# First loads of an attention and FFN kernel in another order, staging of its own at the change of parts, and smaller DMA packets for w_out's forms

## The chip, the cores and the metric

One core of a Trainium2 chip runs the whole program. TensorE (PE) multiplies, VectorE (DVE) and ScalarE (ACT) work on tiles element by element, GpSimd (POOL) sets constants, SyncE (SP) issues most DMAs; 16 DMA engines move the data between HBM and SBUF. Times are device microseconds (us) of one execution. The kernel before took 885.45, 887.29 and 890.8 us, median 887.29.

## The reference

Linear attention without softmax, an RMS norm over each head's 64 values, and a feed-forward layer:

```python
kv = np.einsum('bhsd,bhse->bhde', k, v)          # q, k, v: 8 batches x 8 heads x 576 x 64
out = np.einsum('bhsd,bhde->bhse', q, kv)
rms = np.sqrt(np.mean(out * out, axis=-1, keepdims=True) + 1e-06)
x = (out / rms * g_norm), heads side by side      # 4608 tokens x 512
h = x @ w_in                                      # w_in 512 x 2048
g = h * np.tanh(np.log1p(np.exp(h)))              # mish
y = g @ w_out                                     # w_out 2048 x 512
```

`w_in` and `w_out` arrive as float64 and are joined to float32 on the chip from their two 32-bit words.

## The kernel before

Every float32 product is three passes over a high and a low part in `float32r` (`split`: ACT casts, DVE subtracts). Both FFN products are cut into two by two blocks that need seven products instead of eight; A11, S1, S2, S4, A12, S3, A22 are the seven left forms, T1 to T4 and B11, B21, B22 the right ones.

**Part 1** goes over 9 tiles of 512 tokens. For each it loads q, multiplies it with the batch's k/v matrix, normalizes (giving x), makes the forms of x, and multiplies with w_in in 4 groups (n = 0 to 3) of 7 products. Mish of the result goes to a DRAM tile `gd`. Meanwhile it loads k and v of the coming batches (`k_load`, in pairs p of heads, two staging tiles in turn), and makes the forms of w_out, which wait in the DRAM tiles `wod`. **Part 2** goes over 18 groups of 256 tokens: loads g from `gd`, makes its forms, and multiplies with the forms of w_out (`wo`, eight tiles that take the places of w_in's). The first of these groups is multiplied in four quarters, each with two of the eight tiles, since these arrive one after the other.

**What sets the order.** One product is one slot; a table (`at(t, f)`, run by `slot`) says behind which slot's product each other step is issued, `then` puts an eviction ahead of a product. Tile i's group n begins at slot 28 i + 7 n. Each engine runs its instructions in that order, each DMA queue too. All DMAs of SP and ACT share eight landing semaphores in turn, so each DMA also waits until the one eight before it has landed (the waits DMAHW0 to DMAHW7 in the rows below).

**The start** (lines 588 to 645) is written out by hand. w_in comes in 8 groups j of 512 KB x 2; `weights(j, LOAD, SCALE, JOIN, DIFF, BLOCKS, SUMS)` are the steps of one. Raw words wait in a tile `w64` (groups 0, 4, 7) or in a place of w_in's own (`wf5`, `wf6`, `wf7`; groups 5 and 6 reuse the places of 2 and 3, so their loads wait until DVE has joined these). The rows of q of tile 0 (`rows_load`, 4 loads of 1,024 pieces of 256 bytes), k and v of batch 0 (`kv_first`, two halves) and g_norm (`gcol`) are loaded between them on SP. The units u = 0, 1 of tile 0 (four heads each) are transposed by PE from these rows, copied (`turned`), projected, squared, summed and normalized.

**The change of parts.** At slot 6 of the last tile part 1's pools close; at slots 7 and 8 the first two groups of g are loaded, at 10, 17, 24 and 28 two w_out tiles each (a row of `wod` is 14,336 bytes in one piece per partition). ACT stores the last tile's results (`ula`, `ulb`, `ur`: the blocks 11, 21 and the right half, two buffers of each); in all tiles before, SP does. At slot 18 all seven forms of g's first quarter are made at once, in tiles of their own (`g0`).

## Time and profile before

| | |
|---|---|
| median of 3 runs | 887.29 us (885.45 to 890.8) |
| profiled execution | 885.97 us, span 884.2 us |
| granted TensorE clock, mean | 0.987 |
| PE busy | 828.1 us (94% of the span) |
| DVE, ACT busy | 608.7 us (69%), 464.6 us (53%) |
| DMA | 175.52 MB, mean 199 GB/s |

In a row of the timeline stand the start and length in us, the engine, the line, the operation, what it writes and reads, how many instructions were merged (x), and in brackets the engine's idle time before it with what ended it. SPq and ACTq are DMA issues. q1 is SP's DMA queue, q10 ACT's; behind them stand packets, MB and the time that the packets took as a share of 16 engines' time. PE is TensorE's multiplications. Part 1 ends with the product before 512 us, part 2 follows.

### The profile page before, as it was taken

What the parts mean: (1) busy time and instruction counts of PE and PEld (TensorE: products, weight loads), DVE (VectorE), ACT (ScalarE), POOL (GpSimd) and SP (SyncE); (2) the same over time, 40 slices, a digit from 0 to 9 for tenths busy, and PEclk for the clock granted to TensorE, in tenths of its full rate; (3) what the DMA queues carried; (4) which work ended last, traced back from release to release, by engine and by line L of the source; (5) the groups of instructions that cost most, each with busy time, mean ns of one, the idle gap of its engine ahead of it and who ended that gap; (6) DMA issues with size and microseconds to landing.
All of it is one profiled execution on the core that took longest, in us unless ns stands there. A gap on an engine that the chain in (4) does not pass through costs nothing.

```text
span 884.2 us, 17156 instructions
## 1 busy us (share of the span) xinstructions
PE 828.1 (94%) x7036; PEld 795.7 (90%) x7036; DVE 608.7 (69%) x804; ACT 464.6 (53%) x703; POOL 4.8 (1%) x23
## 2 busy tenths in 40 slices
PE   4658998998999999999999899999999999999997
PEld 3447898998999999999999789999999999999997
DVE  5869675886777676787764368867777677776772
ACT  3647666556675765666664444344444434434431
POOL 2000000000000000000000000000000000000000
PEclk9969999999999999999999999999999999999999
DMA  9936787987978696767477993344434443334421
GB/s 294 247 114 197 200 274 246 278 263 226 296 219 278 218 304 199 220 204 227 151 227 249 425 416 125 122 150 152 148 121 133 130 120 120 119 120 141 153 65 48
DMA packets 161038, 175.52 MB, mean 199 GB/s; under 512 B 24704, under 2 KB 142464, under 8 KB 159936
## 3 DMA queue, kind: packets, MB, share of 16 engines
q1 hardware_dynamic: 158208, 170.23, 61.8%
q10 hardware_dynamic: 2752, 4.20, 1.3%
q8 instruction: 55, 0.90, 0.4%
q14 instruction: 23, 0.19, 0.1%
HBM read 112.39 MB, written 62.00 MB: 197 GB/s over the span
## 4 chain that ended last, share of the span: by engine, by line
PE 63%; DMA 11%; DVE 10%; ACT 9%; issue 4%; SPq 2%; ACTq 0%; DVEq 0%
PE a L772 22%; PE bc L772 16%; PE a L527 13%; PE bc L527 7%; DMA gd<-ula 5%; PE s L252 2%; DMA vm<-in_v_dram 2%; DVE ur L548 1%; DMA wod<-wst 1%; ACT L412 1%; ACT gf L121 1%; DMA rd<-fl 1%; DVE gf L122 1%; DVE fa L122 1%; ACT L118 1%
## 5 line engine op out<-in xcount | busy, mean ns | idle before, releaser
L772 PE MATMUL a<-wf,gf 128*128 128x256 f32 x1632 | 201.8, 283 | 0.5 <-DVE ur L812 0.5
L772 PEld LDWEIGHTS a<-wf,gf 128*128 128x128 f32 x1632 | 198.4, 192 | 0.7 <-DVE ur L812 0.7
L122 DVE TENSOR_TENSOR gf<-g,gf 128x1024 fp32r<-128x1024 f32 (+1 forms) x123 | 132.9, 1087 | 90.7 <-ACT gf L121 90.7
L527 PE MATMUL a<-gf,wf 128*128 128x256 f32 x1296 | 173.0, 287 | 11.5 <-DVE gf L430 4.5
L527 PEld LDWEIGHTS a<-gf,wf 128*128 128x128 f32 x1296 | 162.9, 193 | 18.1 <-ACT ur L504 6.6
L527 PE MATMUL bc<-gf,wf 128*128 128x256 f32 x1296 | 170.3, 285 | 3.5 <-ACT ur L495 2.4
L527 PEld LDWEIGHTS bc<-gf,wf 128*128 128x128 f32 x1296 | 161.4, 191 | 5.1 <-ACT ur L495 2.6
L121 ACT CAST gf<-g 128x1024 fp32r<-128x1024 f32 (+1 forms) x123 | 114.6, 939 | 93.3 <-DVE g L752 65.1
L772 PE MATMUL bc<-wf,gf 128*128 128x256 f32 x1224 | 152.7, 283 | 1.0 <-DVE gf L122 1.0
L772 PEld LDWEIGHTS bc<-wf,gf 128*128 128x128 f32 x1224 | 149.4, 192 | 1.4 <-ACT gf L121 0.7
L527 PE MATMUL a<-a,wf 128*128 128x256 f32 x432 | 59.8, 289 | 2.5 <-DVE ur L548 2.5
L527 PEld LDWEIGHTS a<-a,wf 128*128 128x128 f32 x432 | 55.8, 195 | 5.6 <-DVE ur L548 3.1
L118 ACT ACTIVATE ur<-ur 128x1024 f32<-128x1024 f32 x36 | 38.1, 1059 | 37.1 <-DVE ur L548 37.1
L122 DVE TENSOR_TENSOR fa<-fl,fh 128x1024 fp32r<-128x1024 f32 x28 | 34.3, 1224 | 22.1 <-ACT fh L121 21.2
L504 ACT COPY ur<-a 128x512 f32<-128x512 f32 (+1 forms) x53 | 27.3, 516 | 37.6 <-PE a L772 24.6
L122 DVE TENSOR_TENSOR gf<-gf 128x512 fp32r<-128x512 f32 x45 | 30.4, 689 | 24.0 <-ACT gf L121 24.0
L121 ACT CAST gf<-a 128x1024 fp32r<-128x1024 f32 x17 | 17.9, 1052 | 53.5 <-DVE a L749 50.9
L121 ACT CAST gf<-gf 128x512 fp32r<-128x512 f32 x45 | 27.1, 618 | 31.4 <-DVE gf L451 19.1
L495 ACT COPY ur<-bc 128x512 f32<-128x512 f32 (+1 forms) x53 | 27.4, 517 | 29.9 <-PE bc L772 23.0
L548 DVE TENSOR_TENSOR ula<-bc,ula 128x512 f32<-128x512 f32 x36 | 24.8, 688 | 25.4 <-PE bc L527 25.3
L118 ACT ACTIVATE ula<-ula 128x512 f32<-128x512 f32 x36 | 22.8, 633 | 22.1 <-DVE ula L548 22.1
L252 PE MATMUL s<-vm,km 128*64 128x64 f32 x448 | 20.1, 235 | 14.1 <-DMA vm<-in_v_dram 14.1
(137 smaller groups left out, 858.1 us busy)
## 6 DMA issues: line engine op xcount, KB each, us to landing
g<-gd SPq DMA_DIRECT2D x18, 2048.0 KB, 8.9
gd<-ur SPq DMA_DIRECT2D x32, 512.0 KB, 4.0
wod<-wst SPq DMA_DIRECT2D x16, 896.0 KB, 5.6
wf<-wod SPq DMA_DIRECT2D x8, 1792.0 KB, 16.2
gd<-ula SPq DMA_DIRECT2D x32, 256.0 KB, 5.1
gd<-ulb SPq DMA_DIRECT2D x32, 256.0 KB, 4.3
w<-in_moe_w_out_dram SPq DMA_DIRECT2D x32, 256.0 KB, 4.6
km<-in_k_dram SPq DMA_DIRECT2D x28, 256.0 KB, 4.8
```

The source lines that it names most:

```text
L118: nc.scalar.activation(o, i, AF.Mish)
L121: nc.scalar.copy(hi, src)
L122: nc.vector.tensor_sub(lo, src, hi.bitcast(F32))
L252: nc.tensor.matmul(kvps[o * D:(o + 1) * D, b % 2, h0 // 2 + i, :], kt, vt, start=(c == 0), stop=(c == CM))
L412: nc.scalar.preload_act_table_set("natural_log_exp_and_others")
L495: then(t + 2, lambda: nc.scalar.copy(dst(st, "22"), st["c"]))
L504: then(t + 4, lambda: nc.scalar.copy(dst(st, "12"), st["a"]))
L527: nc.tensor.matmul(bank[:, jj], w[:, right, a, kc, :], xf[:, b, kc, :], start=first and jj == kc == s == 0, stop=(kc == 1 and s == 2), ski ...
L548: nc.vector.tensor_add(o, bank, o)
L772: nc.tensor.matmul(bank, gf[:, a, c, :], wo[c][:, right, b, :], start=first and c == s == 0, stop=(c == NF2 - 1 and s == 2), skip_group_ch ...
```

## The change

It has five places. (1) w_in's groups 6 and 7 are loaded two slots later, group 4 only behind the rows of tile 1. (2) q's rows of tile 0 are issued by ACT and g_norm by POOL, and at the start `turned` of unit 1 and the first k/v product with `kv_keep` move ahead. (3) The last group of the last tile gets staging of its own (`up2`). (4) The forms of g's first quarter are made one per slot, 17 to 23, in rooms of the common pool. (5) A row of `wod` gets 64 bytes behind its two halves of each form, so that w_out's forms are read in 7 pieces of 2,048 bytes per partition; each half of `wod`'s forms is stored in two DMAs.

```diff
@@ -109,7 +109,7 @@
     ones = const.tile([P, P], F32, name="ones")
     sel = const.tile([P, NKC, H], F32R, name="sel")
     gd = [tc.dram_tile([P, NFC, T], F32, name=f"gd{i}") for i in range(NT)]
-    wod = [tc.dram_tile([P, 7, 2, G], F32, name=f"wod{c}") for c in range(NF2)]
+    wod = [tc.dram_tile([P, 7, 2 * G + 16], F32, name=f"wod{c}") for c in range(NF2)]
     rd = [tc.dram_tile([H, T], F32, name=f"rd{j}") for j in range(NT)]
 
     ctx.enter_context(tc.manual_schedule(engines=None))
@@ -197,7 +197,8 @@
             return pools["w64"].tile([P, 4, P, 2], U32, name="w64")
 
         def store(f):
-            nc.sync.dma_start(wod[c][:, :, :, h * P:(h + 1) * P], f.rearrange("p f s m n -> p f s (m n)").bitcast(F32))
+            for s in range(2):
+                nc.sync.dma_start(wod[c][:, :, s * G + h * P:s * G + (h + 1) * P], f[:, :, s, 0, :].bitcast(F32))
         srcs = []
         for fh in range(2):
             f0 = (c + fh * NF2) * P
@@ -286,13 +287,13 @@
             segs.append((j, 0, slice(n, T)))
         return segs
 
-    def rows_load(j, c):
+    def rows_load(eng, j, c):
         for b, s0, cols in segments(j):
             t0, t1 = max(cols.start, c * P), min(cols.stop, (c + 1) * P)
             if t0 < t1:
                 src = q[b, 0:1, s0 + t0 - cols.start:s0 + t0 - cols.start + 1, :]
                 src = bass.AP(src.tensor, src.offset, [[D, t1 - t0], [S * D, H], [1, D]])
-                nc.sync.dma_start(rows[j][t0 - c * P:t1 - c * P, c, :].rearrange("p (h d) -> p h d", d=D), src)
+                eng.dma_start(rows[j][t0 - c * P:t1 - c * P, c, :].rearrange("p (h d) -> p h d", d=D), src)
 
     rows = {}
     qs, ss = {}, {}
@@ -534,7 +535,8 @@
 
         name, shape = {"11": ("la", TH), "21": ("lb", TH)}.get(block, ("r", T))
         if name not in st:
-            st[name] = up.tile([P, 2, shape], F32, name="u" + name)
+            pool = pools["up2"] if (st["i"], st["n"]) == (NT - 1, NQ - 1) else up
+            st[name] = pool.tile([P, 2, shape], F32, name="u" + name)
         return st[name] if name != "r" else st[name][:, :, (int(block[0]) - 1) * TH:int(block[0]) * TH]
 
     def put_in(st, block, bank, t):
@@ -590,15 +592,14 @@
     t = wfp.tile([P, 3, 2 * T], F32, name="wf2")
     rows[0], turned_q = t[:, 0:2].rearrange("p a (c n) -> p (a c) n", c=TR // 2), t[:, 2].rearrange("p (a t) -> p a t", a=2)
     for c in range(TR):
-        rows_load(0, c)
+        rows_load(nc.scalar, 0, c)
     kv0 += [wfp.tile([P, NKC, 9 * D], F32, name=f"wf{n}") for n in (3, 4)]
     kv_first(first)
     weights(1, LOAD)
     kv_first(second)
     for r in (slice(0, D), slice(D, P)):
-        nc.sync.dma_start(gcol[r, :], g_norm.rearrange("(p o) -> p o", o=1))
+        nc.gpsimd.dma_start(gcol[r, :], g_norm.rearrange("(p o) -> p o", o=1))
     weights(2, LOAD)
-    weights(4, LOAD)
     weights(3, LOAD)
     make_identity(nc, ident)
     kv_tiles()
@@ -616,11 +617,11 @@
     do(0, 1, "transpose")
     weights(0, BLOCKS)
     do(0, 0, "turned")
+    do(0, 1, "turned")
     weights(0, SUMS)
-    do(0, 1, "turned")
-    weights(1, SCALE, JOIN)
     kv_first_product(first)
     kv_keep(0, first)
+    weights(1, SCALE, JOIN)
     do(0, 0, "project", "square")
     weights(1, DIFF, BLOCKS)
     kv_first_product(second)
@@ -633,7 +634,7 @@
     k_load(1, 1)
     rows[1] = att.tile([P, TR, H * D], F32, name="qs")
     for c in range(TR):
-        rows_load(1, c)
+        rows_load(nc.sync, 1, c)
     do(0, 1, "square", "sums")
     weights(2, SCALE)
     do(0, 0, "normalize")
@@ -642,6 +643,7 @@
     do(0, 1, "rstd", "normalize")
     x_form(S1)
     weights(2, DIFF)
+    weights(4, LOAD)
     weights(5, LOAD)
 
 
@@ -651,7 +653,7 @@
     for j in range(3, NF2):
         t = 3 * (j - 3) + 1
         if j < 5:
-            at(t, lambda j=j: weights((6, 7)[j - 3], LOAD))
+            at(t + 2, lambda j=j: weights((6, 7)[j - 3], LOAD))
         for s, n in ((SCALE, 0), (JOIN, 0), (DIFF, 1), (BLOCKS, 1), (SUMS, 2)):
             at(t + n, lambda j=j, s=s: weights(j, s))
 
@@ -713,17 +715,17 @@
 
     def part2():
         part1.close()
-        open_pools(ctx, ("gp", 2), ("fp2", 1), ("g0", 1))
+        open_pools(ctx, ("gp", 2), ("fp2", 1), ("g0", 1), ("up2", 1))
         pools["ps"] = ctx.enter_context(tc.tile_pool(name="ps_u", bufs=1, space=PSUM, reuse_waits="tile"))
 
     def gf_room():
         nonlocal rooms_made
         rooms_made += 1
-        return (fp if rooms_made % 5 != 1 else pools["fp2"]).tile([P, 4, 2, 2, P], F32R, name="gf")
+        return (fp if rooms_made % 5 != 2 else pools["fp2"]).tile([P, 4, 2, 2, P], F32R, name="gf")
 
     def wo_load(c):
         wo[c] = wfp.tile([P, 7, 2, G], F32R, name=f"wf{c}")
-        nc.sync.dma_start(wo[c].bitcast(F32), wod[c])
+        nc.sync.dma_start(wo[c].bitcast(F32).rearrange("p f s n -> p f (s n)"), wod[c][:, :, 0:2 * G])
 
     def g_load(s):
         g = gs[s]["g"] = pools["gp"].tile([P, NFC, G], F32, name="g")
@@ -812,8 +814,6 @@
             nc.vector.tensor_add(o, bank, o)
 
     def pair_rooms(n):
-        if n == 0:
-            return [pools["g0"].tile([P, m, 2, 2, P], F32R, name=f"g{m}") for m in (4, 3)]
         return [gf_room() for _ in range(2)]
 
 
@@ -821,7 +821,13 @@
     at(t8 + 6, part2)
     at(t8 + 7, lambda: g_load(0))
     at(t8 + 8, lambda: g_load(1))
-    at(t8 + 18, lambda: g_pair(gs[0], 0, pair_rooms(0)))
+    first_rooms = []
+    for n, f in enumerate(MADE):
+        def first_form(f=f):
+            if f == MADE[0]:
+                first_rooms.extend(pair_rooms(0))
+            gs[0]["f"][f, 0] = g_form(gs[0], f, slice(0, 2), first_rooms[f // 4][:, f % 4])
+        at(t8 + 17 + n, first_form)
     for n in range(NQ - 1):
         for m in range(2):
             at(t8 + 7 * n + 10, lambda c=2 * n + m: wo_load(c))
```

Three places where the order of instructions changes. First SP's queue from the start; before (w64 and wf5 are w_in's groups 0 and 1, wf2 is q's rows, wf3 and wf4 are k and v, gcol is g_norm):

```order
L137 DMA w64_136<-in_moe_w_in_dram 128x4x256 x2
L295 DMA wf2_139<-in_q_dram 128x8x64 x4
L226 DMA wf3_144<-in_k_dram 128x2x576
L226 DMA wf4_145<-in_v_dram 128x2x576
L137 DMA wf5_148<-in_moe_w_in_dram 128x4x256 [waits DMAHW0_49]
L137 DMA wf5_148<-in_moe_w_in_dram 128x4x256 [waits DMAHW1_49]
L226 DMA wf3_144<-in_k_dram 128x2x576 [waits DMAHW2_49]
L226 DMA wf4_145<-in_v_dram 128x2x576 [waits DMAHW3_49]
L599 DMA gcol_88<-in_g_norm_dram 64x1 [waits DMAHW4_49]
L599 DMA gcol_88<-in_g_norm_dram 64x1 [waits DMAHW5_49]
L137 DMA wf6_155<-in_moe_w_in_dram 128x4x256 [waits DMAHW6_49]
```

and now, with the rows of q on ACT's queue, ahead of its first work:

```order
L137 DMA w64_136<-in_moe_w_in_dram 128x4x256 x2
L227 DMA wf3_144<-in_k_dram 128x2x576
L227 DMA wf4_145<-in_v_dram 128x2x576
L137 DMA wf5_148<-in_moe_w_in_dram 128x4x256 [waits DMAHW0_49]
L137 DMA wf5_148<-in_moe_w_in_dram 128x4x256 [waits DMAHW1_49]
L227 DMA wf3_144<-in_k_dram 128x2x576 [waits DMAHW2_49]
L227 DMA wf4_145<-in_v_dram 128x2x576 [waits DMAHW3_49]
L137 DMA wf6_155<-in_moe_w_in_dram 128x4x256 [waits DMAHW4_49]
```

```order
L590 ACT_TABLE_LOAD
L296 DMA wf2_139<-in_q_dram 128x8x64 x4
L142 ACTIVATE fl_186<-w64_136 128x1024 [waits DMAHW2_49,DMAHW0_49]
L121 CAST wf0_214<-fl_186 128x256 [waits DVE_49]
L121 CAST wf0_214<-fl_186 128x2x256
L339 COPY fh_219<-x2_195 128x1024 [waits PE_49]
L121 CAST wf0_214<-wd_191 128x4x256 [waits DVE_49]
L270 COPY kvf0_165<-s2_123 64x2x64 [waits PE_49,Pool_49]
```

k and v stand directly behind group 0; ACT issues four loads before it scales group 0 (L142), and the copies of the k/v matrix (L270) stand ahead of the scaling of group 1.

Second, SP's queue from the loads of groups 5 (wf6) and 6 (wf7) on, with k and v of batch 1 (km, kr, vm, vr) behind them; before:

```order
L137 DMA wf6_387<-in_moe_w_in_dram 128x4x256 [waits DMAHW1_49,DVE_49,Activation_49]
L137 DMA wf6_387<-in_moe_w_in_dram 128x4x256 [waits DMAHW2_49]
L137 DMA wf7_441<-in_moe_w_in_dram 128x4x256 [waits DMAHW3_49,DVE_49,Activation_49]
L137 DMA wf7_441<-in_moe_w_in_dram 128x4x256 [waits DMAHW4_49]
L213 DMA km_459<-in_k_dram 128x2x256 [waits DMAHW5_49,PE_49]
L214 DMA kr_460<-in_k_dram 64x2x64 [waits DMAHW6_49,PE_49]
L213 DMA vm_461<-in_v_dram 128x2x256 [waits DMAHW7_49]
L214 DMA vr_462<-in_v_dram 64x2x64 [waits DMAHW0_49]
```

and now:

```order
L137 DMA wf6_387<-in_moe_w_in_dram 128x4x256 [waits DMAHW7_49,DVE_49,Activation_49]
L137 DMA wf6_387<-in_moe_w_in_dram 128x4x256 [waits DMAHW0_49]
L214 DMA km_456<-in_k_dram 128x2x256 [waits DMAHW1_49,PE_49]
L215 DMA kr_457<-in_k_dram 64x2x64 [waits DMAHW2_49,PE_49]
L214 DMA vm_458<-in_v_dram 128x2x256 [waits DMAHW3_49]
L215 DMA vr_459<-in_v_dram 64x2x64 [waits DMAHW4_49]
L214 DMA km_498<-in_k_dram 128x2x256 [waits DMAHW5_49,PE_49]
L215 DMA kr_499<-in_k_dram 64x2x64 [waits DMAHW6_49,PE_49]
L214 DMA vm_500<-in_v_dram 128x2x256 [waits DMAHW7_49]
L215 DMA vr_501<-in_v_dram 64x2x64 [waits DMAHW0_49]
L137 DMA wf7_522<-in_moe_w_in_dram 128x4x256 [waits DMAHW1_49,DVE_49,Activation_49]
L137 DMA wf7_522<-in_moe_w_in_dram 128x4x256 [waits DMAHW2_49]
```

Group 6 went behind both pairs of k and v (its two rows are now the last); the two loads of group 4 (w64) stand directly ahead of these rows.

Third, ACT's queue in the last tile's groups 1 and 2 (g4, g3 and gf hold forms of g; ula, ulb, ur are the staging tiles, gd8 their store); before:

```order
L504 COPY ur_5664<-a_5634 128x2x256 [waits PE_49]
L121 CAST g4_5711<-g_5537 128x256 [waits DMAHW7_49]
L121 CAST g4_5711<-g1_5715 128x256 [waits DVE_49]
L121 CAST g4_5711<-g_5537 128x256 [waits DVE_49]
L121 CAST g3_5712<-g_5537 128x256 [waits DMAHW0_49]
L121 CAST g4_5711<-g_5537 128x256 [waits DVE_49]
L121 CAST g3_5712<-g_5537 128x256 x2
L546 DMA gd8_103<-ulb_5678 128x2x256 [waits DMAHW2_49,Activation_49]
L118 ACTIVATE ula_5648<-ula_5648 128x512 [waits DVE_49]
L118 ACTIVATE ur_5664<-ur_5664 128x1024 [waits DVE_49]
L490 COPY ula_5775<-a_5761 128x512 [waits DMAHW6_49,PE_49]
L551 DMA gd8_103<-ula_5648 128x2x256 [waits DMAHW3_49,Activation_49]
```

and now:

```order
L121 CAST gf_5711<-g_5556 128x256 [waits DMAHW5_49]
L556 DMA gd8_103<-ur_5577 128x1024 [waits Activation_49]
L505 COPY ur_5683<-a_5653 128x2x256 [waits PE_49]
L121 CAST gf_5711<-g1_5734 128x256 [waits DVE_49]
L121 CAST gf_5711<-g_5556 128x256 [waits DVE_49]
L548 DMA gd8_103<-ulb_5697 128x2x256 [waits DMAHW0_49,Activation_49]
L118 ACTIVATE ula_5667<-ula_5667 128x512
L121 CAST gf_5712<-g_5556 128x256
L121 CAST gf_5711<-g_5556 128x256 [waits DVE_49]
L118 ACTIVATE ur_5683<-ur_5683 128x1024
L491 COPY ula_5790<-a_5773 128x512 [waits PE_49]
L121 CAST gf_5712<-g_5556 128x256
```

The casts of the first quarter's forms, in one piece before, now stand between the last groups' steps, and the copy into the last ula waits for no store.

## The prediction, made before the result

> **What bounds the kernel now.** I read the stretches of the span first, then the waits of the two stretches in which PE stands still, then the DMA traffic there. The stretches (from:to, length, then busy time of PE, PEld, DVE, ACT and POOL, granted clock, DMA share, GB/s):
>
> ```profile
> 0.00:58.00 58.00, 27.52 (x277) 20.15 (x278) 37.49 (x52) 26.68 (x40) 4.76 (x23) 0.86 0.88 245
> 58.00:480.00 422.00, 409.12 (x3519) 386.10 (x3519) 302.75 (x454) 274.57 (x431) 0.00 (x0) 0.99 0.76 229
> 480.00:550.00 70.00, 62.80 (x509) 61.23 (x508) 39.34 (x73) 28.29 (x55) 0.00 (x0) 1.00 0.86 340
> 550.00:880.00 330.00, 328.64 (x2737) 328.23 (x2735) 229.12 (x226) 135.04 (x177) 0.00 (x0) 1.00 0.39 122
> ```
>
> PE is the bound: it is idle for 56 of 884 us, of which 30.5 lie in the first 58 us, 12.9 spread over part 1, 7.2 in the change of parts and 1.4 in part 2. The change can win in the first and the third stretch. The head:
>
> ```profile
> 1.79 5.30 SPq L295 DMA_DIRECT2D wf<-in_q_dram  x4
> 10.99 1.33 PE L325 MATMUL x<-ident,wf 128*128 128x128 f32 x5 [0.60 <-DMA wf<-in_q_dram]
> 14.35 2.39 PE L234 MATMUL s<-wf,wf 64*64 64x64 f32 x72 [0.32 <-DMA wf<-in_v_dram]
> 17.32 1.12 ACT L142 ACTIVATE fl<-wf 128x1024 f32<-128x1024 f32 x1 [3.01 <-DMA wf<-in_moe_w_in_dram]
> 18.34 0.51 ACT L269 COPY kvf<-s 64x128 f32<-64x128 f32 x2
> 18.47 0.69 DVE L147 TENSOR_SCALAR fl<-fl 128x1024 uint32<-128x1024 uint32 x1 [1.71 <-ACT fl L142]
> 34.23 2.31 PE L527 MATMUL a<-gf,wf 128*128 128x256 f32 x12 [4.54 <-DVE gf L430]
> 35.19 12.57 SPq L137 DMA_DIRECT2D wf<-in_moe_w_in_dram  x4
> 36.47 1.12 PE L252 MATMUL s<-vm,km 128*64 128x64 f32 x16
> 37.52 0.48 PE L252 MATMUL s<-vr,kr 64*64 64x64 f32 x4
> 47.86 0.45 SPq L213 DMA_DIRECT2D km<-in_k_dram  x1
> 51.73 1.22 DVE L122 TENSOR_TENSOR wf<-wd,wf 128x1024 fp32r<-128x1024 f32 x1
> 54.62 1.12 PE L252 MATMUL s<-vm,km 128*64 128x64 f32 x16 [12.88 <-DMA vm<-in_v_dram]
> 60.69 0.69 DVE L147 TENSOR_SCALAR fl<-fl 128x1024 uint32<-128x1024 uint32 x1 [7.74 <-ACT fl L142]
> ```
>
> The last row of q lets the transposes go on at 10.99; the first FFN product starts at 34.23; then PE waits 12.88 us for k and v of batch 1. Their load stands on SP behind w_in group 6 (in the x4 from 35.19 to 47.76), which waits until DVE has joined group 3.
>
> **Change 1, group 6 loaded two slots later.** SP then reaches the load of k and v (pair 2) as soon as its staging tile is free, that is when PE has finished pair 0: 37.52 + 0.48 = 38.0, 3.8 us after the first product. From the load's issue to PE's start it took 54.62 - 47.86 = 6.8 us, so PE goes on 10.6 us after its first product and not 20.4: 9.8 us won at most. But DVE is in order and had work until 51.73 + 1.22 = 52.95; then it was idle for 7.74 us, since ACT stood behind a copy that waited for PE. DVE loses only that idle time, and PE needs DVE's forms: I take 7.7 (7.7 to 9.8). The load of group 4, moved behind the rows of tile 1, has its data long before slot 4 and costs nothing.
>
> **Change 2, q's rows from ACT's queue.** SP loses four issues (5.30 us in all), and k, v and w_in now travel beside q. What that does depends on how the DMA engines share two queues. The trace has such a stretch, ACT's stores beside SP's loads of w_out forms, and rows that price the packets:
>
> ```profile
> DMA packets 1191, 8.51 MB, mean 425 GB/s; under 512 B 96, under 2 KB 561, under 8 KB 659
> q1 hardware_dynamic: 595, 7.61, 89.1%
> q10 hardware_dynamic: 595, 0.88, 11.7%
> ...
> DMA packets 774, 0.76 MB, mean 381 GB/s; under 512 B 34, under 2 KB 774, under 8 KB 774
> ...
> DMA packets 2607, 0.66 MB, mean 219 GB/s; under 512 B 2607, under 2 KB 2607, under 8 KB 2607
> ...
> DMA packets 318, 0.70 MB, mean 387 GB/s; under 512 B 16, under 2 KB 16, under 8 KB 318
> ```
>
> The first three rows are 500 to 520 us: SP's queue (q1) and ACT's (q10) moved 595 packets each, though q1's are 14,336 bytes and q10's 1,024 or 4,096. They take turns packet by packet, whatever the size. The others are 3 to 5 us (w_in, 740 packets of 1,024 bytes in 2 us: 43 ns each on 16 engines), 6 to 9 us (q, 256 bytes: 18 ns) and 11 to 12.8 us (k and v, 302 of 2,304 bytes: 95 ns).
>
> q has 4 x 1,024 packets. In turns they pass one SP packet each: 1,024 of w_in group 0, 512 of k and v, 1,024 of group 1, 512 of k and v, 1,024 of group 2, exactly 4,096. That takes 3,072 x (43 + 18) / 16 + 1,024 x (95 + 18) / 16 = 11.7 + 7.2 = 19 us; the same prices give 7.4 us for the old order (group 0, then q), which ended at 10.99, so some 3 us of start and landing come on top. PE sees the last row near 22: +11.0. The landing waits of the order (each DMA waits for the one eight before it) tie SP's later loads to q's rows and change that little. The transposes behind that row (3.0 us, 10.99 to 14.03), the k/v product, `kv_keep` and the projection follow on PE in order.
>
> `kv_keep` now stands ahead of the scaling of group 1 on ACT and no longer waits for it; but the scaling then comes behind: transposes to 25.0, k/v product 2.4, `kv_keep` 0.5 and its hand-overs to 28.0, scaling 1.1, and DVE's L147 starts at 29.2, 10.7 later than 18.47. From there to 34.23 DVE's chain is in order (group 1, both normalizations), so the first product comes near 44.9. Price of change 2: +10.7, with bounds of -2 (q lands as before, k and v a little earlier) and +11.5. The two copies of u1 and group 0's last subtraction change places on DVE ahead of group 1, which needs neither sooner: nothing. g_norm on POOL's queue: POOL is busy for 4.76 us of this stretch, and the first normalization comes late in it; covered.
>
> [...]
>
> Head: +10.7 - 7.7 = **+3.0** (+0.9 with 9.8; -9 to -12 if q is not late).
>
> **Changes 3 to 5, the change of parts.** Pieces of the chain of waits, PE's waits, and the traffic from 476 to 527 and from 527 to 531:
>
> ```profile
> 486.30 14.09 DMA gd<-ula
> 500.55 23.00 DMA gd<-ula
> ...
> 497.39 1.69 PE L527 MATMUL bc<-gf,wf 128*128 128x256 f32 x12 [1.11 <-DVE ula L548]
> 501.11 1.70 PE L527 MATMUL a<-gf,wf 128*128 128x256 f32 x12 [0.59 <-ACT ula L490]
> 506.60 1.70 PE L527 MATMUL bc<-gf,wf 128*128 128x256 f32 x12 [2.36 <-ACT ur L495]
> 510.52 1.70 PE L527 MATMUL a<-a,wf 128*128 128x256 f32 x12 [0.78 <-DVE ur L548]
> 512.05 5.20 PE L863 MATMUL q<-wf,g 128*128 128x256 f32 x42
> 528.28 0.98 PE L863 MATMUL q<-wf,gf 128*128 128x256 f32 x6 [0.60 <-DVE gf L122]
> 529.98 4.21 PE L863 MATMUL q<-wf,gf 128*128 128x256 f32 x33 [0.72 <-DVE gf L122]
> 534.03 3.04 PE L772 MATMUL a<-wf,gf 128*128 128x256 f32 x24
> 543.30 3.10 PE L772 MATMUL bc<-wf,gf 128*128 128x256 f32 x24 [0.48 <-DVE gf L122]
> ...
> 476.00:527.00 51.00, 46.15 (x378) 45.34 (x378) 20.48 (x47) 20.69 (x43) 0.00 (x0) 1.00 1.03 415
> ...
> q10 hardware_dynamic: 925, 1.27, 85.2%
> q1 hardware_dynamic: 18, 0.07, 4.4%
> ```
>
> Own staging, a form per slot and quicker stores take away the first four waits, 4.8 us, so PE enters the first product of part 2 at 507 and not 512. But the DMA engines are full from 476 to 527 (share 1.03), and the last eighth of that product needs w_out group 7, the last of these transfers, which has 18 packets left at 527 and lands at about 528. Before, PE used it from some 531.5 (21 products of 5.20 / 42 us before 534.03): 3.5 us of slack. That transfer gets later. ACT's stores, no longer starved, go ahead of it: the 1.27 MB that now follow it cost 1.27 / 415 = 3.1 us. And the eight loads, 14.68 MB, ran at 7.61 MB in 89.1% of 20 us, 427 GB/s; packets of 2,048 bytes are not in the trace. By their bytes alone nothing is lost; at the rate of the 2,304-byte packets, 387 GB/s, 3.5 us are. I take 2.6, nearer the second row. Group 7 lands at 528 + 5.7 = 533.7, and PE's last eighth starts 2.2 us later (0 to 3.1). While PE waits, DVE gets ahead with the next forms, so the wait of 543.30 and its like behind it go, 1.0 in all. Price: **+1.2** (-1.0 to +3.1). The 4.8 us do not turn into a cost; they are spent in front of a full DMA.
>
> ACT's stores also wait for landings eight DMAs back: ulb of group 1 for w_out group 0, ulb of group 2 for w_out group 2. These land later now, with stores between their packets, and ACT stands there with the evictions behind it; up to 5 us of that are covered by the wait for group 7. The first quarter's forms take rooms of the shared pool; the first is the tile of x, free since slot 3 of the last tile.
>
> `wod` in two stores: 16 more issues on SP, at 0.45 us (L213 above) 7 us if all lay on the path. The chain of the whole page has few of them:
>
> ```profile
> PE a L772 22%; PE bc L772 16%; PE a L527 13%; PE bc L527 7%; DMA gd<-ula 5%; PE s L252 2%; DMA vm<-in_v_dram 2%; DVE ur L548 1%; DMA wod<-wst 1%; ACT L412 1%; ACT gf L121 1%; DMA rd<-fl 1%; DVE gf L122 1%; DVE fa L122 1%; ACT L118 1%
> ```
>
> So it is one issue or less: **+0.3**.
>
> **Sum.** The profiled execution took 885.97 us (span 884.2), 1.3 below the median of the runs, inside their scatter. 885.97 + 3.0 + 1.2 + 0.3 = 890.5: against the median 887.29, +0.4%, just short of the 0.5% (4.4 us) that a measurement of this kernel can tell from no change. Own range 886 to 895.
>
> **Rivals.** *q is not late* (faster). If one turn carried several 256-byte packets, q would get its share in bytes and land by 11; the first product then comes 1 us earlier, since k, v and group 1 no longer wait for q's issues: -1 - 7.7 + 1.2 + 0.3 = -7.2, 878.8 (876 with 9.8 and -2). It decides as soon as q's last row lands before some 15 us. For it: no row shows 256-byte packets on one queue beside larger ones on the other. Against it: 595 to 595, where q10's 1,024-byte packets came two to a partition.
>
> [...]
>
> *The change of parts wins its stalls* (no change). If group 7 doesn't hold PE, 4.8 + 1.3 + 1.0 of its waits go: 3.0 + 0.3 - 7.1 = -3.8, 882.2. For it: the chain runs through gd<-ula for 37 us. Against it: share 1.03, and only 3.5 us of slack at the end.
>
> *ACT stands behind landings* (slower). If the stores' waits hold ACT for more than the 5 us, the forms of the second, third and fourth quarter come late, by some 2 us each (as 506.60 waited 2.36 on ACT): 4.5 + 6 = 10.5, 896.5. Against it: ACT is busy for 20.69 of those 51 us.
>
> **Chances.** Late q with the full DMA: 0.62; it straddles the bound, same 0.29, slower 0.31, faster 0.02. q not late: 0.25, all but 0.01 faster. Stalls won: 0.08, faster 0.03, same 0.05. ACT behind landings: 0.05, slower. Together faster 0.29, same 0.35, slower 0.36. The range, 877.5 to 895, leaves out a tenth on each side.
>
> **What would show it.** The transposes of tile 0 waiting on q until near 22, first product near 45, k and v's wait in slot 2 down from 12.88 to some 3 us, DVE's 7.74 gone. In the change of parts: gd<-ula landing in under 6 us, no wait on staging, and PE waiting for wf<-wod in the last quarter. Wrong if the transposes end before 15 us, or if PE reaches part 2's second group earlier, counted from slot 7 of the last tile, than now.

## The result and the profile after

The changed kernel took 894.78 us (median of 9 executions, 891.84 to 897.12) against 887.29 (885.45 to 890.8): a ratio of 1.0081, 95% interval 1.0063 to 1.0100. It is slower by 7.5 us. The profiled execution took 891.84 us (span 890.1), 5.9 more than the one of before; the two profiles account for that part, and the other 1.6 us are the distance of both to their medians.

Two stretches of the span after (from:to, length, busy time of PE, PEld, DVE, ACT, POOL, granted clock, DMA share, GB/s):

```profile
0.00:58.00 58.00, 28.13 (x279) 20.90 (x280) 30.95 (x43) 22.93 (x34) 5.95 (x25) 0.94 0.78 226
480.00:550.00 70.00, 62.40 (x490) 61.12 (x489) 37.80 (x70) 28.67 (x56) 0.00 (x0) 0.95 0.97 357
```

In the second of these the DMA share went from 0.86 to 0.97 and the clock from 1.00 to 0.95. The head, from the timeline after, beside the same rows of the prediction (q's last row 10.99, first FFN product 34.23, k and v 12.88 late at 54.62):

```profile
23.26 1.33 PE L326 MATMUL x<-ident,wf 128*128 128x128 f32 x5 [3.57 <-DMA wf<-in_q_dram]
30.12 1.14 ACT L142 ACTIVATE fl<-wf 128x1024 f32<-128x1024 f32 x1
46.67 2.93 PE L528 MATMUL a<-gf,wf 128*128 128x256 f32 x12 [4.54 <-DVE gf L431]
55.70 0.69 PE L253 MATMUL s<-vm,km 128*64 128x64 f32 x16 [0.60 <-DMA vm<-in_v_dram]
65.34 0.69 DVE L147 TENSOR_SCALAR fl<-fl 128x1024 uint32<-128x1024 uint32 x1
65.99 3.58 PE L361 MATMUL x<-fh,kvf 128*128 128x448 f32 x6 [2.95 <-ACT kvf L270]
```

q's last row comes 12.3 us later and the first FFN product 12.4 us later; the wait of 12.88 us for k and v is down to 0.60, so that PE is level with the kernel before at 62.7 us. But DVE is not: it won back only its 7.74 us of idle time, and L147 of w_in group 4 comes 4.7 us later (65.34 against 60.69). PE then waits 2.95 us for ACT's next copy of the k/v matrix, a wait that the kernel before did not have, and by the transposes of tile 1 it is 4.7 us late too (76.42 against 71.75). Some 1.2 us of that come back in the rest of part 1: SP issued the first load of g at 475.78; before it did so at 472.34 (its row "472.34 2.29 SPq L731", the same load), 3.4 us earlier. That is what the head cost. The change of parts, from the timeline after:

```profile
475.78 2.92 SPq L733 DMA_DIRECT2D g<-gd  x2
500.72 0.63 ACT L118 ACTIVATE ula<-ula 128x512 f32<-128x512 f32 x1 [3.81 <-DMA wf<-wod]
502.76 1.69 PE L528 MATMUL a<-a,wf 128*128 128x256 f32 x12 [1.59 <-DVE ur L550]
504.96 1.69 PE L528 MATMUL a<-gf,wf 128*128 128x256 f32 x12 [0.51 <-ACT ula L491]
511.14 0.63 ACT L118 ACTIVATE ula<-ula 128x512 f32<-128x512 f32 x1 [3.67 <-DMA wf<-wod]
511.75 1.70 PE L528 MATMUL a<-a,wf 128*128 128x256 f32 x12 [0.78 <-DVE ur L550]
528.75 3.84 PE L869 MATMUL q<-wf,gf 128*128 128x256 f32 x21 [2.70 <-DMA wf<-wod]
533.96 4.03 PE L869 MATMUL q<-wf,gf 128*128 128x256 f32 x21 [1.37 <-DMA wf<-wod]
538.63 2.78 PE L869 MATMUL q<-wf,gf 128*128 128x256 f32 x21 [0.64 <-DMA wf<-wod]
541.25 3.04 PE L774 MATMUL a<-wf,gf 128*128 128x256 f32 x24
```

No engine waits for the store of a staging tile any more, but PE still has three waits there, 2.9 us together (502.76, 504.96 and 511.75), where it had four of 4.8. The first two stand behind ACT, which waited 3.81 us for a landing of w_out's forms; a wait like the last, 0.78 or 0.79 us, is there in all kernels below. So PE enters part 2's first product 37.5 us after the load of g (513.29 - 475.78) and not 39.7 (512.05 - 472.34): 2.2 us are won and not 4.8. There PE waits three times for w_out's forms, 4.7 us in all, and the second group of part 2 starts 65.5 us after the load of g (541.25 - 475.78) where it started 61.7 us after it (534.03 - 472.34): 3.8 us. The waits of 543.30 and 546.96 are gone, so 2.5 us of these stay at the end of the span (5.9 less 3.4).

DMA queues of the changed kernel, first from 10 to 14 us (q beside w_in, k and v), then from 500 to 520 (ACT's stores beside w_out's forms); packets, MB, share of 16 engines:

```profile
q1 hardware_dynamic: 922, 1.11, 84.6%
q10 hardware_dynamic: 921, 0.23, 26.6%
...
q1 hardware_dynamic: 3250, 6.56, 86.4%
q10 hardware_dynamic: 1011, 1.36, 18.4%
```

The turns can be seen one by one in the packets' times: in the kernel before, from 500 to 520 us, a data packet of SP's starts within 4 ns of the end of 513 of ACT's 563 data packets, and in 42 cases one of ACT's alone. So one piece went in a turn here.

### The profile page after: what moved, and what is told of

Same layout as the page of the kernel before. It is cut to its first block, busy times and chain, and to the rows that moved or that the text cites. A ratio compares the mean times of both kernels' runs of the same rounds, so it can differ in the third digit from the quotient of the medians.

```text
span 890.1 us, 17179 instructions
## 1 busy us (share of the span) xinstructions
PE 831.8 (93%) x7036; PEld 799.2 (90%) x7036; DVE 609.3 (68%) x804; ACT 465.3 (52%) x703; POOL 6.0 (1%) x25
## 4 chain that ended last, share of the span: by engine, by line
PE 68%; DMA 11%; ACT 8%; DVE 7%; issue 4%; SPq 1%; ACTq 0%; DVEq 0%
PE a L774 22%; PE bc L774 17%; PE a L528 14%; PE bc L528 8%; DMA wf<-wod 4%; PE s L253 3%; DMA wf<-in_q_dram 2%; DVE ur L550 1%; DMA vm<-in_v_dram 1%; ACT L413 1%; PE q L869 1%; DMA rd<-fl 1%; DVE fa L122 1%; DMA gd<-ula 1%; DMA fa<-rd 1%
## 5 line engine op out<-in xcount | busy, mean ns | idle before, releaser
L122 DVE TENSOR_TENSOR gf<-g,gf 128x1024 fp32r<-128x1024 f32 (+1 forms) x130 | 135.9, 1052 | 104.0 <-ACT gf L121 103.9
L121 ACT CAST gf<-g 128x1024 fp32r<-128x1024 f32 (+1 forms) x130 | 117.3, 910 | 87.8 <-DVE g L754 67.4
L550 DVE TENSOR_TENSOR ur<-bc,ur 128x512 f32<-128x512 f32 x36 | 24.4, 678 | 7.8 <-ACT ur L505 4.3
```

The source lines that it names most:

```text
L121: nc.scalar.copy(hi, src)
L122: nc.vector.tensor_sub(lo, src, hi.bitcast(F32))
L550: nc.vector.tensor_add(o, bank, o)
```

## The experiments

Each kernel below computes all of the reference. Ratios are to the kernel before, run beside each; "base" in a diff is the kernel that the text names.

### q's rows back on SP

```diff
-    rows_load(nc.scalar, 0, c)      # base: the changed kernel
+    rows_load(nc.sync, 0, c)
```

> The changed kernel with one edit undone: q's rows of tile 0 are issued by SP again, between w_in group 0 and the first k and v; all else of the change stays. Theory (q shares the DMA engines packet by packet with SP's loads): q's last row lands near 11 us again and not at 23.26, the first FFN product starts near 34 and not at 46.67, so the time falls by 10.7 to 12.4 us, to 882.4 to 884.1. Rival (q's queue is not what holds the head; the issues on ACT or the new order of DVE and ACT do): the last row lands early but the first product still starts after 40, and the time stays above 889.

Measured: 883.9 us, ratio 0.9962 (0.9945 to 0.9978), 10.6 us below the changed kernel by the ratios: as expected. q's last row and the first product:

```profile
11.24 1.33 PE L326 MATMUL x<-ident,wf 128*128 128x128 f32 x5 [0.46 <-DMA wf<-in_q_dram]
34.74 2.93 PE L528 MATMUL a<-gf,wf 128*128 128x256 f32 x12 [4.54 <-DVE gf L431]
```

With this one edit the changed kernel would have been faster than before. q's queue is what held the head: the first load of g stands at 464.66 in this kernel, 11.1 us ahead of the changed one and 7.7 ahead of before.

### Only q's rows on ACT

```diff
-        rows_load(0, c)             # base: the kernel before
+        rows_load(nc.scalar, 0, c)
```

> The kernel before with one edit: q's rows of tile 0 are issued by ACT. Theory: last row near 22 to 23, first product near 45 to 47, and the time rises by the 10.7 us of the sum to 898 (12.4, the shift seen in the changed kernel, would give 899.7); the 12.88 us wait for k and v in slot 2 stays, since the load of group 6 ahead of them moves with DVE's chain. Rival (part of the delay is taken up by the wait for k and v, which does not move with it): 888 to 894.

Measured: 893.41 us, ratio 1.0067 (1.0048 to 1.0086): +5.9 us, inside the rival's 888 to 894 and not the theory's 898 to 900.

```profile
20.36 1.33 PE L325 MATMUL x<-ident,wf 128*128 128x128 f32 x5 [1.81 <-DMA wf<-in_q_dram]
41.66 2.93 PE L527 MATMUL a<-gf,wf 128*128 128x256 f32 x12 [4.54 <-DVE gf L430]
61.65 1.12 PE L252 MATMUL s<-vm,km 128*64 128x64 f32 x16 [11.57 <-DMA vm<-in_v_dram]
```

The first product is only 7.4 us later (41.66 - 34.23), and the wait for k and v takes up 1.3 of these (11.57 instead of 12.88). In the changed kernel q cost 11.9 us at the first product (46.67 - 34.74). So something else in the head's edits makes a late q dearer: the next but one section finds it.

### Only groups 6 and 7 later

```diff
-            at(t, lambda j=j: weights((6, 7)[j - 3], LOAD))      # base: the kernel before
+            at(t + 2, lambda j=j: weights((6, 7)[j - 3], LOAD))
```

> The kernel before with one edit: w_in groups 6 and 7 are loaded two slots later. Theory: the wait of 12.88 us for k and v in slot 2 falls to some 3 to 5 us, DVE's idle 7.74 us behind it is gone, and the time falls by 7.7 to 9.8 us, to 877.5 to 879.6. Rival (something else, group 6 itself or the k and v of the next pair, is late in their place): the time falls by less than 3 us, and a new wait of 5 us or more stands between 55 and 100 us.

Measured: 880.15 us, ratio 0.9912 (0.9893 to 0.9932): 7.8 us won by the ratio, 7.2 between the medians. It beats both kernels, and the wait for k and v fell to 2.76, where 3 to 5 were expected.

```profile
33.95 2.93 PE L527 MATMUL a<-gf,wf 128*128 128x256 f32 x12 [4.54 <-DVE gf L430]
44.93 0.69 PE L252 MATMUL s<-vm,km 128*64 128x64 f32 x16 [2.76 <-DMA vm<-in_v_dram]
```

### The head's other two edits, each undone in the changed kernel

```diff
-        nc.gpsimd.dma_start(gcol[r, :], ...)      # first kernel: g_norm on SP again
+        nc.sync.dma_start(gcol[r, :], ...)
...
-    do(0, 1, "turned")                            # second kernel: the order of before
     weights(0, SUMS)
+    do(0, 1, "turned")
+    weights(1, SCALE, JOIN)
     kv_first_product(first)
     kv_keep(0, first)
-    weights(1, SCALE, JOIN)
```

> The changed kernel with one edit undone: g_norm's two loads are issued by SP again, behind the second k and v, and not by POOL. With q on ACT alone (kernel before plus that one edit) q's last row was used at 20.36 us and the first FFN product started at 41.66; in the changed kernel 23.26 and 46.67. Theory (g_norm's loads stood 5.05 us on SP there, waiting for a landing, and held SP's w_in group 2 back, so that q met fewer SP packets): q's last row comes 2 to 3 us earlier, near 20.5, and the time falls by 2 to 3 us, to about 892. Rival (g_norm's place is nothing): last row within 0.7 us of 23.26, and 894 to 895.

> The changed kernel with one edit undone: in the head, the scaling and joining of w_in group 1 stand ahead of the first k/v product again, and the sums of group 0 ahead of the second copy of u1. Theory (this order costs nothing with an early q, but with a late one ACT scales group 1 only at 30.12, behind kv_keep's copy, and DVE's chain of group 1 follows): the scaling goes to near 25.6, the first product comes 2 to 4 us before 46.67, and the time falls by 2 us, to 892.5 to 893. Rival (the order is nothing): first product within 0.7 us of 46.67, and 894 to 895.

Measured: 890.77 us, ratio 1.0054 (1.0038 to 1.0070), and 892.1 us, ratio 1.0069 (1.0054 to 1.0084). Timeline rows of the first, then of the second:

```profile
13.29 5.03 SPq L601 DMA_DIRECT2D gcol<-in_g_norm_dram  x2
20.28 1.33 PE L326 MATMUL x<-ident,wf 128*128 128x128 f32 x5 [1.94 <-DMA wf<-in_q_dram]
42.95 2.93 PE L528 MATMUL a<-gf,wf 128*128 128x256 f32 x12 [3.60 <-DVE gf L431]
```

```profile
26.52 1.17 ACT L142 ACTIVATE fl<-wf 128x1024 f32<-128x1024 f32 x1
44.76 2.93 PE L528 MATMUL a<-gf,wf 128*128 128x256 f32 x12 [4.56 <-DVE gf L431]
```

g_norm's place is worth 3.7 us at the first product (46.67 - 42.95), 3.0 of them in q's last row (23.26 to 20.28); the order is worth 1.9 (46.67 - 44.76), with q's row where it was (23.30) and the scaling of group 1 at 26.52 instead of 30.12. With q's 7.4 alone these make 13.0, and 12.4 were measured: the head's loss is accounted for. By the times they are worth 2.4 and 1.1 us, with intervals that overlap the changed kernel's; the rows carry them (the first product of kernels with the same head differs by 0.3 us, 33.95 to 34.23). Of g_norm's place 2 to 3 us were expected in q's last row, and 3.0 came; of the order 2 to 4 us at the first product, and 1.9 came.

How g_norm on POOL delays q can be seen. Queues of the changed kernel, then of the one with g_norm on SP, each from 6 to 10 us and from 19 to 23:

```profile
q1 hardware_dynamic: 632, 1.07, 76.7%
q10 hardware_dynamic: 547, 0.14, 15.7%
q0 software_dynamic: 62, 0.00, 1.0%
...
q1 hardware_dynamic: 1224, 1.36, 102.4%
q10 hardware_dynamic: 136, 0.03, 4.2%
```

```profile
q1 hardware_dynamic: 701, 1.21, 88.7%
q10 hardware_dynamic: 704, 0.18, 22.2%
...
q1 hardware_dynamic: 908, 0.76, 69.5%
q10 hardware_dynamic: 290, 0.07, 8.1%
```

While POOL's 62 packets go (4 or 16 bytes each), q moves 157 packets fewer in these 4 us. But that is not what costs the time: by 19 us the changed kernel has moved 4,024 packets of ACT's queue and the other one 3,870. What costs it is the end. q's last packets, 136 in the changed kernel, trickle out over some 3.5 us beside nine times as many of SP's, while in the other kernel 290 are through before 20 us.

The packets' times give a reason, as an estimate. The last 100 of q's packets in the changed kernel take 2.7 us, 27 ns each, and 98 of them are followed within 5 ns by one of SP's, of which one starts every 3.3 ns there (1,224 in 4 us), so that this alone shows no turn. A packet of each in turn takes 18 + 43 = 61 ns by the prediction's prices, so by this estimate only some two of the 16 DMA engines still have q to move, each in turns with SP: 136 / 2 turns of 61 ns are 4.1 us, and on 16 engines they would be 0.5. In the other kernel the last 100 take 0.2 us, and none has a packet of SP's right behind it. The kernel with the old order, which has g_norm on POOL too, is like the first (2.7 us and 97), and the one with only q on ACT like the second (0.3 us and none). Why two engines would be behind where POOL's few packets went is open, and the expectation's own reason, that g_norm's waiting loads (5.03 us on SP) hold group 2 back from q, is there as well: with g_norm on SP both go, and no run parts them.

### q's rows on both queues, and on POOL's

```diff
-        rows_load(0, c)             # base of both: the kernel with groups 6 and 7 later
+        rows_load(nc.scalar if c < 2 else nc.sync, 0, c)     # first kernel
+        rows_load(nc.gpsimd, 0, c)                           # second: each row in two loads
```

> The kernel before with w_in groups 6 and 7 two slots later (880.15 us when timed alone), and with q's rows of tile 0 split: the first two of the four loads are issued by ACT, the last two by SP behind w_in group 0. Theory (queues take turns packet by packet): the 2,048 packets on ACT's queue meet 1,024 of w_in group 0 and then 1,024 of q itself, 1,024 x (43 + 18) / 16 + 1,024 x (18 + 18) / 16 ns = 6.2 us, the other 1,024 of q take 1.2 more; with the 3 us of start and landing the last row comes at 10 to 11.5 us, as with all rows on SP (10.96), and the time is 879 to 881. Rival (a load on ACT's queue is late in itself, whatever SP moves meanwhile): ACT's two rows land after 13 us, the first FFN product starts 2 us or more after 33.95, and the time is 882 or more.

> The kernel before with w_in groups 6 and 7 two slots later (880.15 us), and with q's rows of tile 0 on POOL's queue, the software path, each row in two loads of 512 packets. Theory (packet by packet on this path too): in stretches where both queues have work, POOL's queue and SP's move like numbers of packets, q's last row comes after 20 us, and the time rises by at least 6 us, to 886 or more. [...]

Measured: 879.92 us, ratio 0.9924 (0.9910 to 0.9937), no different from the base; and 910.66 us, ratio 1.0274 (1.0256 to 1.0292). In the first kernel:

```profile
11.56 1.33 PE L325 MATMUL x<-ident,wf 128*128 128x128 f32 x5 [0.64 <-DMA wf<-in_q_dram]
```

A load on ACT's queue was not late in itself here: with two of the four loads on it q's last row came at 11.56, with all on SP at 10.96, and with all on ACT, in the kernel with that edit alone, at 20.36. What fits these times is the turns that SP's packets take between its own (922 to 921 above). The second kernel, its timeline and its packets from 24 to 26 us:

```profile
1.26 0.82 POOL L298 DMA_DIRECT2D wf<-in_q_dram  x1 [0.81 <-POOLq L940]
40.89 0.69 POOL L298 DMA_DIRECT2D wf<-in_q_dram  x1 [2.53 <-issue]
42.21 0.90 PE L328 MATMUL x<-ident,wf 128*128 128x128 f32 x3 [42.21 <-POOL ident masks.py:199]
...
DMA packets 556, 0.64 MB, mean 318 GB/s; under 512 B 32, under 2 KB 524, under 8 KB 556
q0 software_dynamic: 48, 0.13, 23.2%
```

The second expectation missed its reason, though the time is above its 886: not the queues decide here but POOL. It issues the eight loads of 512 pieces 3.2 to 6.7 us apart, and makes the identity for PE's transposes only behind them, so PE's first transpose waits until 42.21. So this run does not tell how fast q would be on POOL's queue. It does show the size of a packet there: the 48 packets hold one whole load, 131,072 bytes; 32 of the 556 packets are over 2 KB, where SP's have 1,024 bytes and less, so POOL's are 4,096 bytes each, sixteen pieces of q (its other 16 have 4 bytes). On SP's and ACT's queues one piece was one packet: of ACT's 921 packets above 905 have the 256 bytes of a piece of q, and of SP's 922 packets 733 have the 1,024 of a piece of w_in.

### The change of parts

Four kernels take changes 3 to 5 apart.

```diff
-    wod = [tc.dram_tile([P, 7, 2 * G + 16], ...)]     # big packets: base is the changed kernel
+    wod = [tc.dram_tile([P, 7, 2, G], ...)]
...
-    wod = [tc.dram_tile([P, 7, 2, G], ...)]           # packets only: base is the kernel before
+    wod = [tc.dram_tile([P, 7, 2 * G + 16], ...)]     # with its two stores per form
...
+            pool = pools["up2"] if (st["i"], st["n"]) == (NT - 1, NQ - 1) else up     # parts alone:
+    at(t8 + 17 + n, first_form)                       # base is the kernel with groups 6 and 7 later
...
-        eng = nc.sync if i < NT - 1 else nc.scalar    # POOL's stores: base is parts alone
+        eng = nc.sync if i < NT - 1 else nc.gpsimd
```

> The changed kernel with one edit undone: the w_out forms lie without the 16 spare elements, so their loads go in packets of 14,336 bytes again (the two stores per form stay). Theory (the small packets and the stores that go ahead share the delay of w_out group 7): group 7 lands 2.6 us (0 to 3.5) earlier than in the changed kernel, the first product of part 2's second group starts 2 to 3 us before 541.25, and the time falls to 892 to 893. Rival 1 (only the stores' share counts; packets of 2,048 bytes cost nothing): no change, 894 to 895. Rival 2 (the small packets let the stores through; in large ones ACT's stores starve, and staging or its landing waits stop PE in the last group of part 1 again): gd<-ula takes over 10 us to land, and the time is 894 or more.

> The kernel before with one edit: w_out's forms are stored with 16 spare elements, in two stores, and loaded in packets of 2,048 bytes; staging and the first forms of part 2 stay as before. Theory (at 380 GB/s, SP's rate in the changed kernel from 500 to 520 us, instead of 427 the 14.68 MB take 4.2 us longer, against 3.5 us of slack; and with seven times as many turns ACT's stores no longer starve, so the waits on staging go and PE comes earlier to the same full DMA): gd<-ula lands in under 8 us, PE waits for wf<-wod in the last eighths of part 2's first product, and the time is 1 to 3 us above before, 888.3 to 890.3. Rival 1 (the packets' price is nothing): within 0.7 us of 887.3. Rival 2 (freed stores win the 4.8 us of waits): 883 to 885.

> The kernel before with w_in groups 6 and 7 two slots later (880.15 us when timed alone) and, of the rest of the change, only the staging of its own and the first forms one per slot; packets of 14,336 bytes, one store per form. Theory (ACT's stores still starve behind the large packets, and now ACT itself stands behind the landings that its later stores wait for, with the forms of the third and fourth quarter behind it): the waits on staging go, gd<-ula lands only after 19 us, PE waits 3 to 5 us for forms made by DVE and ACT in part 2's first product, and the time is 0 to 2.7 us above 880.15. Rival (the staging wins its stalls up to the 3.5 us of slack of w_out group 7): 876.5 to 878.

> The kernel before with w_in groups 6 and 7 two slots later, the staging of its own and the first forms one per slot (that alone: PE waits 4 us for forms in part 2's first product, gd<-ula lands after 17 us and more), and with the stores of the last tile issued by POOL, which has nothing else to do there, and not by ACT. Theory (ACT's waits for landings, 1.7, 3.6 and 2.7 us and one of some 3 behind the third quarter, make the forms late): ACT has no such wait, PE's waits for forms in that product fall below 2 us together, and the time is 2 to 3.5 us below that of the same kernel with the stores on ACT: 876 to 878.5 against 879.2 to 880.4. Rival (w_out group 7 lands no earlier and holds PE instead, or POOL's stores starve so that part 2's first load of results is late): 879 to 881.

Measured, with the time from SP's first load of g to the first product of part 2's second group in the profile of each:

| kernel | us | ratio (interval) | load of g to second group |
|---|---|---|---|
| before | 887.29 | 1 | 61.7 |
| changed | 894.78 | 1.0081 (1.0063 to 1.0100) | 65.5 |
| changed, big packets | 891.45 | 1.0044 (1.0029 to 1.0059) | 64.4 |
| before, small packets only | 889.46 | 1.0036 (1.0022 to 1.0050) | 66.9 |
| groups 6 and 7 later | 880.15 | 0.9912 (0.9893 to 0.9932) | 61.8 |
| that, with staging and forms per slot | 879.22 | 0.9927 (0.9912 to 0.9942) | 62.6 |
| that, with stores by POOL | 881.5 | 0.9937 (0.9924 to 0.9951) | 62.7 |

Small packets cost 3.2 us in the kernel before, with the two stores, and 3.3 in the changed kernel, where the two stores stay, by the ratios. The profiles do not show the second figure: both spans are 890.1 us, that of the changed kernel being its fastest execution, and the one with big packets having lost 2.7 us to the clock (last section). Against what was expected, small packets alone lie inside (888.3 to 890.3), big packets are 0.5 below, with `gd<-ula` slow again (19.6 us) as the second rival said, and staging with forms per slot lies between theory and rival, with the theory's waits for forms (4.5 us together). Staging and forms per slot are worth nothing either way, and POOL's stores nothing more. Rows of the changed kernel with big packets, of small packets only, of staging and forms alone, and of POOL's stores with its queues from 500 to 520 us:

```profile
529.18 0.40 ACT L121 CAST gf<-g 128x256 fp32r<-128x256 f32 x1 [4.16 <-PE q L869]
534.59 6.93 PE L869 MATMUL q<-wf,gf 128*128 128x256 f32 x33 [0.72 <-DVE gf L122]
```

```profile
534.89 3.80 PE L864 MATMUL q<-wf,gf 128*128 128x256 f32 x21 [1.94 <-DMA wf<-wod]
```

```profile
507.33 0.41 ACT L121 CAST gf<-g 128x256 fp32r<-128x256 f32 x1 [2.72 <-DMA gd<-ulb]
```

```profile
520.03 7.99 PE L868 MATMUL q<-wf,gf 128*128 128x256 f32 x42 [2.67 <-DMA wf<-wod]
...
q1 hardware_dynamic: 539, 6.81, 79.7%
q0 software_dynamic: 499, 1.72, 21.2%
```

Here each repair of a wait handed it on. With large packets and more staging, ACT stands behind landings and PE waits for forms. With POOL's stores ACT stands nowhere, but POOL's packets are larger than ACT's (1.72 MB in 499, 3.4 KB in the mean, where ACT's had 1.36 MB in 1,011), the stores get more of the full DMA engines (21.2% of their time instead of the 15.1% in its base), and PE waits for w_out's forms again. The stretch takes 61.7 to 62.7 us in all kernels with large packets, whatever PE waits for, but for the changed one (64.4), where ACT stood for 4.16 us and the last 33 products took 6.93 us instead of the 4.21 of the kernel before (529.98 there). POOL's stores were expected at 876 to 878.5: that theory fell. Its rival's mechanism held (PE waits for w_out), and its range, 879 to 881, was missed by 0.5.

### Two more waits of the best kernel

```diff
-    weights(5, LOAD)                                  # base: groups 6 and 7 later
+    at(2, lambda: weights(5, LOAD))
...
-(1, 8, "transpose"), (1, 9, "turned"), (0, 9, "sums"),
+(1, 9, "transpose"), (0, 9, "sums"), (1, 10, "turned"),
```

> The kernel before with w_in groups 6 and 7 two slots later (880.15 us when timed alone), and two more edits that its waits suggest: w_in group 5 is loaded behind k and v of pair 2 and not ahead of them (PE waited 2.76 us for these at 44.93), and the second half of tile 1's transposes stands one slot later on PE (it waited 4.09 us at 63.68 for ACT, with products behind it that waited for nothing). Theory (both waits stand ahead of free work): the first falls to about 1 us, the second is filled by the product behind it, and the time falls by 2 to 6 us, to 874 to 878. Rival (DVE is behind both, as in the 7.74 us that limited the change to 7.7: what PE gains here it waits for forms a little later): 879 to 881.

Measured: 879.34 us, ratio 0.9909 (0.9891 to 0.9927), the same as its base; the rival held.

```profile
51.06 1.12 PE L252 MATMUL s<-vm,km 128*64 128x64 f32 x16 [4.54 <-DMA vm<-in_v_dram]
```

The wait at 63.68 is gone, that for k and v is halved (1.30 instead of 2.76), and the next pair, now behind group 5, waits 4.54.

## Why the prediction was right, and where it was not

The forecast was 890.5 us and slower by 0.4%; 894.78 lies inside the range, 4.3 us above the forecast and only 0.2 below the range's end. The likeliest case came true in both places: a late q and a full DMA. The sum was added to the profiled execution of 885.97, and the profiled execution after took 891.84, 1.3 above the sum; the other 2.9 us are that execution's distance to the median, which was 1.3 before and which the sum did not count. That the terms come so near is in part luck: some were too large, some were left out, and these errors had opposite signs.

- **Group 6 later, -7.7**: right. Alone it won 7.8 us (6.0 to 9.5 by the interval), near the 7.7 that DVE's idle time allowed. In the profiles the first load of g came 5.5 us earlier with this edit alone and 7.7 earlier in the changed kernel with q back on SP.
- **q on ACT's queue, +10.7**: near as a sum (12.4 at the first product), with its parts mis-sized. The turns are there, packet for packet (922 to 921). q's last row was said to come near 22 and came at 23.26; the first product was said at 44.9 and came at 46.67. But q alone cost 7.4 at the first product, and its last row came at 20.36, earlier than the counting gave. The rest comes from two edits. "g_norm on POOL's queue ... covered" is the step that failed: it looked at POOL's work and at when g_norm is needed, not at what its packets would do to q's and what stood behind it on SP. That was 3.7 us. The order with `kv_keep` ahead of the scaling was rightly put behind the late row, and cost 1.9.
- **Head +3.0**: 3.4 at the first load of g. That DVE gives back only its idle time was right: 12.4 - 7.7 = 4.7, and PE and DVE were 4.7 us late behind it. The 1.2 us that came back later were not in the prediction; that 3.4 is so near 3.0 is luck.
- **Change of parts +1.2**: 2.5 between the profiles. The main mechanism was as said: PE stands in front of the full DMA, in three eighths and not one. One step was wrong: the first four waits, 4.8 us, do not all go. The last was no wait for staging (it stays with staging of its own), and ACT's wait for a landing makes two new ones, so 2.9 us stay and PE is 2.2 us earlier. It cost nothing, since w_out's forms came later than PE either way. The term that was mis-sized is that of the 2,048-byte packets: 2.6 was taken, 3.5 at most. SP's queue moved 6.56 MB in 86.4% of 20 us, 380 GB/s instead of 427, and 14.68 MB take 4.3 us longer. With 4.3 the same sum gives 3.1 + 4.3 - 3.5 of slack = 3.9, and 3.8 were measured before 1.3 come back, 1.0 of them in the waits named. The bound came from packets of 2,304 bytes of another load (387 GB/s), with no room below it.
- **wod in two stores, +0.3**: not seen by itself.
- **q not late** fell with the first rows. **The change of parts wins its stalls** fell: no mixture of changes 3 and 4 made a kernel faster than its base. **ACT behind landings** was there as a mechanism (3.81 and 3.67 us, and PE's waits of 1.59 and 0.51 behind the first), but by the rows it cost the changed kernel little, since PE waited for w_out behind it anyway; no run takes it away alone.

The signs named beforehand came out so: transposes waiting on q until 23.26, first product at 46.67, k and v's wait at 0.60 (some 3 was said), DVE's 7.74 gone, no wait for a staging tile's store (but 2.9 us of other waits of PE in their place), PE waiting for w_out's forms. `gd<-ula` landed in a median of 6.6 us, not under 6.

## What to carry to other kernels

Before a load of many small pieces goes to a second hardware queue, count the pieces that the first queue moves meanwhile: here the two queues took turns one for one (922 packets to 921), so that 256-byte pieces beside 1,024- and 2,304-byte ones got 0.23 of 1.34 MB, and the load that everything waits for should not be the one with the small pieces. In the stretch in which the DMA engines were full (share 1.03 before), waits that were repaired came back as others; only larger packets shortened it (64.4 us instead of 65.5 in the changed kernel, 61.7 instead of 66.9 in the kernel before). When several edits share a stretch, time each alone: one edit of this change was worth 7.8 us and the others spent it twice.

## What the runs showed of the hardware that was not expected

Behind some waits of PE the clock fell, and 21 products then took 4.03 us instead of 2.78. Two stretches of the changed kernel:

```profile
530.00:535.00 5.00, 3.63 (x18) 3.37 (x17) 4.96 (x5) 1.04 (x1) 0.00 (x0) 0.50 1.05 395
535.00:540.00 5.00, 4.36 (x29) 4.15 (x29) 1.70 (x2) 1.40 (x2) 0.00 (x0) 0.81 1.06 366
```

After the wait of 2.70 us that ended at 528.75 the granted clock was 0.50 until about 537, and 21 products took 3.84 and 4.03 us where they take 2.78 at 538.63. In the changed kernel this was hidden, since PE's last eighth waited for w_out all the same. With small packets only, the last eighth itself took 3.80 us (534.89), 1.0 too long, and in the changed kernel with big packets the 6.93 us were 2.7 too long, with the next group right behind: there the clock was on the path (0.85 from 532 to 538 us in the first, 0.66 in the second). A wait of 2.36 us in the kernel before (at 506.60) left the clock at 1.00, as it did with groups 6 and 7 later (at 501.18). With q's rows on both queues the same row, again 2.36 us (at 501.19), had 0.50 behind it, from 503 to 506, and 12 products took 2.76 us instead of 1.60; with only q's rows on ACT it was the same (514.43, 2.65 us instead of 1.70, 0.50 from 516 to 518). So the length of the wait alone did not decide: behind 2.36 us the clock was 1.00 in two kernels and 0.50 in two. What decides no run shows.

POOL's eight issues of 512 pieces of 256 bytes stand 39.6 us apart from first to last, 5.7 in the mean or 11 ns a piece, and the profile shows nothing that POOL waited for between them. On its queue a packet was sixteen such pieces (4,096 bytes), where on ACT's it was one (256).
